# Chunked attention and two feed-forward layers: one written order for every engine up to the end of block 0

## The chip, the core and the metric

One Trainium2 chip, one of its cores. The time is device microseconds of one execution; the result of a comparison is the median of several runs. TensorE (PE) multiplies, VectorE (DVE) and GpSimd (POOL) do elementwise work, ScalarE (ACT) does exponentials, copies and ReLU, SyncE (SP) issues nearly all transfers.

## The reference

Attention over 4 batches, 8 heads, 768 positions of 64 values, in chunks of 32 positions, each of which sees itself, 16 positions to the left, 8 to the right and 8 memory positions. Its output, 3072 tokens by 512, goes through two feed-forward layers (512 to 2048 to 512):

```python
scores = scale * np.matmul(q_c, k_full.transpose(0, 1, 3, 2))
scores = scores - np.max(scores, axis=-1, keepdims=True)
a = np.exp(scores)
a = a / (np.sum(a, axis=-1, keepdims=True) + 1e-09)
out[:, :, c_start:c_end] = np.matmul(a, v_full)
...
h = x @ w_in            # first layer
r = np.maximum(h, 0.0)
g = s * (r * r) + b
x = g @ w_out
...
h = x @ w_in            # second layer, with its own weights
g = h - np.tanh(h)
return (g @ w_out).astype(np.float32)
```

## The kernel before

Everything is float32 in effect. A product of the feed-forward layers is made of three matmuls (`three`, L106 to L109): weights and inputs are split into a high part and a remainder (low part), and high×high, low×high and high×low are added in PSUM. Weights arrive as 64-bit numbers and are converted on chip (`to_f32`, L111): one ACT copy (L116), then three DVE operations (L117, L118, L121). `make_pair` (L288) follows with the high part on ACT (L293) and the low part on POOL (L294).

Attention works on 24 units of 128 tokens. For one unit `scores` (L193) does 32 small matmuls (S), the mask on DVE (L210), the row maximum on DVE (L215), eight exponentials on ACT (L218) and the division (L223, L224, L226), on DVE for units 0 to 3 and on POOL after. `transposes` (L228) turns the weights with eight PE transposes (T) and two ACT copies (L235); `values` (L239) does 32 matmuls (V) and splits the result into the high part `xh` (ACT, L261) and the low part `xl` (DVE, L262).

Four units make a block of 512 tokens; there are six. The up-projection of the first layer takes 16 tiles per block: `up1_tile` (L324) is 12 matmuls of 128x512, a ReLU on ACT (L334) and a scaled square on DVE (L336). After every four tiles `combine` (L338) makes four differences on POOL (L340), and two transfers store the results. The loop at L544 places attention steps between tiles: `att_step(i)` is T of unit i-1, V of unit i-2 and S of unit i. During blocks 1 to 3 and 5 the conversions of `w_out` are emitted (`load_quadrant`, L354). Then come the down-projection (class `Down`), whose seven products cycle through four pairs of PSUM banks, the second up-projection (L644) and a second `Down`.

The order of the work: from L534 on PE follows the program; for the other engines, DMA issues included, a scheduler chooses the order when the program is built, from times that it computes itself. It may bring work of a later block forward. On the chip each engine then takes its instructions strictly in that order, and one that waits holds all behind it.

Of the kernel before, what the change touches and what calls it, by code (L numbers as in the profile page):

```python
# [8 lines left out]
F32 = mybir.dt.float32  # L9
F32R = mybir.dt.float32r  # L10
# [7 lines left out]
P = 128  # L18
# [15 lines left out]


# [6 lines left out]
def tile_chunk_attention_two_ffn(  # L42
# [50 lines left out]
    def bank(k):  # L93
        return pb[:, 512 * k:512 * (k + 1)]
# [16 lines left out]
    def to_f32(z, raw):  # L111
# [4 lines left out]
        nc.scalar.activation(out=z, in_=hi32.bitcast(F32), func=AF.Copy, scale=2.0 ** -112)  # L116
# [76 lines left out]
    def scores(u):  # L193
# [11 lines left out]
        sm = sm_t[u] = new(A_SM[u % 2], 8 * KE, F32, "sm").rearrange("p (h k) -> p h k", h=8)  # L205
# [8 lines left out]
        nmx = small.tile([P, 8], F32, tag="nmx", name="nmx")  # L214
        nc.vector.tensor_reduce(out=nmx, in_=sm, op=ALU.max, axis=AX.X, negate=True)  # L215
        sums = small.tile([P, 8], F32, tag="sums", name="sums")
        for h in range(8):
            nc.scalar.activation(  # L218
                out=sm[:, h, :], in_=sm[:, h, :], func=AF.Exp,
                bias=nmx[:, h:h + 1], scale=1.0, accum_out=sums[:, h:h + 1],  # L220
            )
        rs = small.tile([P, 8, 1], F32, tag="rs", name="rs")
        nc.vector.tensor_scalar_add(sums, sums, 1e-9)  # L223
        nc.vector.reciprocal(out=rs.rearrange("p h o -> p (h o)"), in_=sums)  # L224
        eng = nc.vector if u < UB else nc.gpsimd
        eng.tensor_tensor(out=sm, in0=sm, in1=rs.to_broadcast([P, 8, KE]), op=ALU.mult)  # L226

    def transposes(u):  # L228
        sm = sm_t.pop(u)
        pt = pt_t[u] = new(A_PT[u % 2], 8 * P, F32, "pt").rearrange("p (h q) -> p h q", h=8)  # L230
        for g in range(2):
            ps = bank(2 + g)
            for r in range(4):
                nc.tensor.transpose(out=ps[0:KE, P * r:P * (r + 1)], in_=sm[:, 4 * g + r, :], identity=ident)  # L234
            nc.scalar.activation(  # L235
                out=pt[0:KE, 4 * g:4 * g + 4, :], in_=ps[0:KE].rearrange("p (r q) -> p r q", r=4), func=AF.Copy
            )

    def values(u):  # L239
        tv = v_t.pop(u).rearrange("p (e h d) -> p e h d", e=2, h=8)  # L240
        pt = pt_t.pop(u)
        ps = bank(4)
        for r in range(4):
            for e in range(2):
                for g in range(2):
                    c0 = P * r + QE * e
                    nc.tensor.matmul(  # L247
                        ps[64 * g:64 * g + 64, c0:c0 + QE],
                        lhsT=tv[0:KE, e, 2 * r + g, :], rhs=pt[0:KE, 4 * g + r, QE * e:QE * (e + 1)],
                        start=True, stop=True,  # L250
                    )
        j = u // UB
# [5 lines left out]
        xh, xl = x_t[j]  # L258
        c0 = P * (u % UB)
        xp = ps.rearrange("p (c q) -> p c q", c=KD)  # L260
        nc.scalar.activation(out=xh[:, :, c0:c0 + P], in_=xp, func=AF.Copy)  # L261
        nc.vector.tensor_tensor(  # L262
            out=xl[:, :, c0:c0 + P], in0=xp, in1=xh[:, :, c0:c0 + P].bitcast(F32), op=ALU.subtract
        )

    done = [0]

    def att_part(part, u):
        if 0 <= u < NU:
            {"S": scores, "T": transposes, "V": values}[part](u)  # L270
            if part == "V":
                done[0] = u + 1
                loads_to(u + 3)

    def att_step(i, parts="TVS"):

        for part in parts:
            att_part(part, i - {"S": 0, "T": 1, "V": 2}[part])
# [18 lines left out]
    raws = {}  # L297
    w_loaded, w_made = [0], [0]

    def w1_load():  # L300
        n = w_loaded[0]
        if n < min(8, w_made[0] + 2):
            raws[n] = load_raw(wi1, n, A_RAW[n % 2])
            w_loaded[0] += 1

    def w1_make():
        n = w_made[0]
        if n in raws:
            make_pair(raws.pop(n), A_Z[n % 2], A_W[n], 1, n)
            w_made[0] += 1  # L310

    loads_to(0, spread=True)
    nc.sync.dma_start(out=s_c, in_=s.partition_broadcast(P))
    nc.sync.dma_start(out=b_c, in_=b.partition_broadcast(P))
    make_identity(nc, ident)
    make_masks()
    loads_to(1, spread=True)
    w1_load()
    loads_to(2, spread=True)
    w1_load()  # L320
# [25 lines left out]
    class Down:  # L346


        def __init__(self, src, zmap, smap, whl, stream, ring, load, view, pick, bias, final):
# [3 lines left out]
            self.loaded = 0  # L353
# [136 lines left out]
    def final1(name, g, ps):  # L490
# [44 lines left out]
    w1_make()
    for n, group in enumerate(("S0 S1 S2", "T0 V0 S3", "T1 V1", "T2 S4 V2", "T3 V3")):
        for step in group.split():
            att_part(step[0], int(step[1:]))
        if n:
            w1_load()  # L540
            w1_make()

    thunks = []
    for j in range(NBLK):  # L544
        first = UB * (j + 1) + 2
        steps = [(i, "TVS") for i in range(first, first + UB)] if j + 1 < NBLK else []
        if j == 0:
            steps.insert(0, (first - 1, "TS"))
        at_tile = {16 * n // len(steps): step for n, step in enumerate(steps)}
        for q in range(4):  # L550
            oa, ob = (
                new(A_OT[q % 2][h], 4 * NB, F32, ("oa", "ob")[h]).rearrange("p (s k t) -> p s k t", s=4, k=2)
                for h in range(2)
            )
            for i4, (k, i) in enumerate(((0, 0), (0, 1), (1, 0), (1, 1))):
                if j == 0:
                    w1_load()
                    while w_made[0] <= min(2 * q + k + 1, 7):
                        w1_load()
                        w1_make()  # L560
                up1_tile(j, 2 * q + k + 8 * i, oa[:, 2 * i:2 * i + 2, k, :])
                if 4 * q + i4 in at_tile:
                    att_step(*at_tile[4 * q + i4])
                if (j in (1, 2, 3) and q in (0, 2)) or (j == NBLK - 1 and q in (0, 1)):
                    if i4 == 1:
                        thunks.append(down1.load_quadrant(A_RAW[1 if j == NBLK - 1 else q // 2]))
                    if i4 == 3:
                        thunks.pop()()
                if j == NBLK - 1 and i4 == 0 and q in (1, 2):
                    down1.weights(0, q - 1)  # L570
                    down1.load_to(q - 1)
            combine(*(t.rearrange("p s k t -> p s (k t)") for t in (oa, ob)), nc.gpsimd)
            nc.sync.dma_start(out=o1[j][:, q, 0:3], in_=oa[:, 1:4].rearrange("p s k t -> p s (k t)"))
            nc.sync.dma_start(out=o1[j][:, q, 3:7], in_=ob.rearrange("p s k t -> p s (k t)"))
# [36 lines left out]
    def final2(name, g, ps):  # L611
# [29 lines left out]
        None, final2,  # L641
    )

    for n in range(8):  # L644
        for g in range(NG):
# [6 lines left out]
            for i in range(2):  # L652
                ps = bank2((2 * at_ + i) % 4)
# [93 lines left out]
```

## Time and profile before

| | |
|---|---|
| median of three runs | 1133.98 us (1132.64 to 1134.48) |
| the profiled execution | 1133.25 us; its span, first to last instruction, 1131.5 us |
| busy: PE, DVE, ACT, POOL | 1072.5, 638.5, 488.7, 453.7 us |
| mean granted TensorE clock | 0.98 |
| qk load of one unit, v load, weight load | 640 KB, 384 KB, 1024 KB |

In the rows below, an instruction of the time line begins with its start and its duration in us; then come engine, line, operation, output<-inputs, shapes and count, and in brackets the idle time before it with what ended it. Groups by line give the busy time in us and the mean in ns behind the bar, then idle time before them. PEclk is the granted clock: 1.00 is 2.4 GHz, 0.5 is 1.2 GHz.

### The profile page before, as it was taken

The page shows a single profiled execution, that of the slowest core. Times are in us where ns is not written, and L with a number is a line of the kernel's source. Part 1 is how long each engine was busy: PE and PEld are TensorE (multiplying, and loading weights), DVE is VectorE, ACT ScalarE, POOL GpSimd, SP SyncE. Part 2 cuts the span into 40 slices and gives each one's busy share as a digit, 9 for nine tenths or more (in the row PEclk, how much of TensorE's full clock was granted, in tenths as well). Part 3 has the DMA queues.
Part 4 walks back from the last instruction along what each step waited for, and adds up shares of the span by engine and source line. Part 5 has one row for each costly group of instructions (what it writes and reads, how often), then busy time and mean ns, then how long its engine had stood idle before and what let it go on. Part 6 is the DMA issues. An engine that isn't in the chain of part 4 may idle for free.

```text
span 1131.5 us, 15217 instructions
## 1 busy us (share of the span) xinstructions
PE 1072.5 (95%) x6048; PEld 886.1 (78%) x6048; DVE 638.5 (56%) x610; ACT 488.7 (43%) x863; POOL 453.7 (40%) x296
## 2 busy tenths in 40 slices
PE   4467999999999999999999999999999999999998
PEld 3346888888888888888888788888888888888886
DVE  5987444444455356657778886333322366667654
ACT  5644544444453345445555433222222354444432
POOL 2343444444448734110110158666655852011100
PEclk9678999999999999999999999999999999999999
DMA  8665755555545675655655686655544885567661
GB/s 306 223 224 197 260 204 205 205 205 212 189 189 211 243 263 186 202 186 187 204 202 189 223 268 237 238 205 197 224 164 168 307 282 201 186 207 251 237 215 56
DMA packets 71686, 242.15 MB, mean 214 GB/s; under 512 B 5312, under 2 KB 5312, under 8 KB 61376
## 3 DMA queue, kind: packets, MB, share of 16 engines
q1 hardware_dynamic: 71280, 240.01, 59.3%
q10 hardware_dynamic: 336, 1.18, 0.3%
q8 instruction: 47, 0.77, 0.3%
q14 instruction: 23, 0.19, 0.1%
HBM read 146.80 MB, written 94.37 MB: 213 GB/s over the span
## 4 chain that ended last, share of the span: by engine, by line
PE 88%; DVE 6%; DMA 3%; ACT 2%; issue 1%; POOL 0%; SPq 0%; POOLq 0%; ACTq 0%
PE pb L107 28%; PE pb L109 28%; PE pb L108 28%; DMA raw<-in_wo_dram 2%; PE pb L247 2%; DVE z L118 1%; PE pb L234 1%; PE pb L201 1%; ACT sm L218 1%; DMA qk<-in_qk_dram 1%; DVE z L121 1%; DVE z L117 1%; ACT zq L116 1%; DVE sm L210 1%; DVE nmx L215 0%
## 5 line engine op out<-in xcount | busy, mean ns | idle before, releaser
L109 PE MATMUL pb<-ringhringl,whl 128*128 128x512 f32 x560 | 218.0, 389 | 0.0
L107 PE MATMUL pb<-ringhringl,whl 128*128 128x512 f32 x560 | 217.9, 389 | 0.0
L108 PE MATMUL pb<-ringhringl,whl 128*128 128x512 f32 x560 | 217.9, 389 | 0.0
L431 DVE TENSOR_TENSOR ringhringl<-part,ringhringl 128x1024 fp32r<-128x1024 f32 x92 | 129.0, 1404 | 84.1 <-ACT ringhringl L430 83.8
L340 POOL TENSOR_TENSOR ob<-oa 128x512 f32<-128x512 f32 x96 | 136.4, 1422 | 65.0 <-DVE oa L660 40.0
L430 ACT ACTIVATE ringhringl<-part 128x1024 fp32r<-128x1024 f32 x92 | 97.7, 1061 | 135.5 <-PE pb L109 122.6
L107 PE MATMUL pb<-xh,w 128*128 128x512 f32 x384 | 153.0, 399 | 2.0 <-ACT xh L261 1.7
L109 PE MATMUL pb<-xl,w 128*128 128x512 f32 x384 | 150.8, 393 | 2.9 <-DVE xl L262 2.9
L108 PE MATMUL pb<-xh,w 128*128 128x512 f32 x384 | 150.6, 392 | 0.0
L109 PEld LDWEIGHTS pb<-ringhringl,whl 128*128 128x128 f32 x560 | 105.1, 188 | 22.3 <-DVE ringhringl L426 0.3
L336 DVE SCALAR_TENSOR_TENSOR oa<-pb,s_c,r 128x512 f32<-128x512 f32 x96 | 70.4, 748 | 92.2 <-ACT r L334 87.9
L108 PEld LDWEIGHTS pb<-ringhringl,whl 128*128 128x128 f32 x560 | 105.1, 188 | 21.9
L107 PEld LDWEIGHTS pb<-ringhringl,whl 128*128 128x128 f32 x560 | 105.1, 188 | 21.7
L660 DVE TENSOR_TENSOR oa<-pb,r 128x1024 f32<-128x1024 f32 x48 | 58.4, 1220 | 110.3 <-ACT r L659 101.6
L659 ACT ACTIVATE r<-pb 128x1024 f32<-128x1024 f32 x48 | 49.1, 1025 | 132.8 <-PE pb L109 128.8
L334 ACT ACTIVATE r<-pb 128x512 f32<-128x512 f32 x96 | 54.8, 589 | 103.7 <-PE pb L109 103.7
L412 POOL TENSOR_TENSOR whl<-s,whl 128x1024 fp32r<-128x1024 f32 x16 | 41.5, 2592 | 135.1 <-ACT whl L411 135.1
L218 ACT ACTIVATE sm<-sm,nmx 128x96 f32<-128x96 f32 x192 | 69.2, 362 | 60.0 <-DVE nmx L215 60.0
L426 DVE SCALAR_TENSOR_TENSOR ringhringl<-part,b_c,ringhringl 128x1024 fp32r<-128x1024 f32 x48 | 71.4, 1494 | 37.5 <-ACT ringhringl L425 37.5
L340 POOL TENSOR_TENSOR ob<-oa,ob 128x512 f32<-128x512 f32 x48 | 64.1, 1336 | 66.6 <-DVE oa L660 45.7
L107 PE MATMUL pb<-x2hx2l,w 128*128 128x512 f32 x224 | 87.3, 390 | 2.4 <-DVE sumU L498 2.4
L107 PEld LDWEIGHTS pb<-xh,w 128*128 128x128 f32 x384 | 72.6, 189 | 19.5 <-ACT xh L261 1.9
(100 smaller groups left out, 1888.3 us busy)
## 6 DMA issues: line engine op xcount, KB each, us to landing
o<-ob SPq DMA_DIRECT2D x48, 1024.0 KB, 5.2
part<-o SPq DMA_DIRECT2D x84, 512.0 KB, 4.5
part<-o SPq DMA_DIRECT2D x42, 1024.0 KB, 5.1
o<-oa SPq DMA_DIRECT2D x48, 768.0 KB, 3.3
raw<-in_wi_dram SPq DMA_DIRECT2D x16, 1024.0 KB, 5.9
raw<-in_wo_dram SPq DMA_DIRECT2D x16, 1024.0 KB, 6.1
qk<-in_qk_dram SPq DMA_DIRECT2D x24, 640.0 KB, 6.9
v<-in_vw_dram SPq DMA_DIRECT2D x21, 384.0 KB, 3.5
```

Source lines behind the costliest of these rows:

```text
L107: nc.tensor.matmul(acc, lhsT=whi, rhs=xhi, start=first, stop=False)
L108: nc.tensor.matmul(acc, lhsT=wlo, rhs=xhi, start=False, stop=False)
L109: nc.tensor.matmul(acc, lhsT=whi, rhs=xlo, start=False, stop=last)
L218: nc.scalar.activation(out=sm[:, h, :], in_=sm[:, h, :], func=AF.Exp, bias=nmx[:, h:h + 1], scale=1.0, accum_out=sums[:, h:h + 1],)
L334: nc.scalar.activation(out=r, in_=ps, func=AF.Relu)
L336: nc.vector.scalar_tensor_tensor(out=dst, in0=ps2, scalar=s_c[:, 0:1], in1=r2, op0=ALU.mult, op1=ALU.mult)
L340: sub = lambda o, x, y: eng.tensor_tensor(out=o, in0=x, in1=y, op=ALU.subtract)
L426: nc.vector.scalar_tensor_tensor(out=xl, in0=src, scalar=self.bias, in1=xh.bitcast(F32), op0=ALU.add, op1=ALU.subtract)
L430: nc.scalar.activation(out=xh, in_=src, func=AF.Copy)
L431: nc.vector.tensor_tensor(out=xl, in0=src, in1=xh.bitcast(F32), op=ALU.subtract)
L659: nc.scalar.activation(out=r, in_=ps[:, :, 0:NB], func=AF.Tanh)
L660: nc.vector.tensor_tensor(out=oa[:, 2 * i:2 * i + 2], in0=ps[:, :, 0:NB], in1=r, op=ALU.subtract)
```

## The change

Up to the end of block 0 every engine follows one written list, `START`. Its tokens name a step and a unit, weight piece, tile or group: `qk`, `vv`, `ra` load; `S M R E D` are scores, mask, maximum, exponentials, division; `T C V X L` are transposes, their copies, values, `xh` and `xl`; `z o h l` are the four stages of a weight piece (ACT copy, three DVE operations, high part, low part); `F r Q` are a tile's products, ReLU and square; `K st` are the combination and its stores. The list holds attention units 0 to 7 whole; the scores of units 8 and 9 and the transposes of unit 8, which stood in block 0 before, come in block 1.

With it: low parts of the first layer's `w_in` go from POOL to DVE; divisions of units 4 to 7 too; of block 0's four combinations the first two go to DVE. The first five qk loads have buffers of their own, and v loads are issued by SP (before, the first three by ACT). Block 1 holds six attention steps, at tiles 0, 2, 5, 8, 11 and 14. The conversions of `w_out` are emitted in blocks 2 to 4 and 5. The second layer's PSUM bank pairs are moved on by one (`turn`).

```diff
+START = """
+qk0 qk1 qk2 S0 M0 qk3 R0 S1 M1 E0 qk4 R1 S2 M2 ra0 E1 S3 D0 R2 M3 vv0 E2 D1 S4 ra1 T0 R3 M4 C0 D2
+vv1 z0 T1 R4 V0 qk5 C1 o0 T2 X0 z1 vv2 E3 qk6 L0 o1 V1 vv3 S5 X1 ra2 C2 L1 D3 V2 ra3 X2 M5 T3 L2 S6
+C3 R5 h0 V3 M6 vv6 l0 X3 h1 vv5 L3 z2 R6 F0 E4 l1 o2 F1 r0 z3 D4 h2 ra4 F2 r1 Q0 E5 o3 F3 qk7 r2 l2
+vv4 Q1 T4 r3 ra5 D5 h3 F4 E6 Q2 Q3 l3 F5 K0 z4 C4 F6 r4 o4 r5 st0 T5 r6 Q4 h4 S7 Q6 z5 V4 Q5 F7 l4
+ra6 o5 F8 qk8 D6 h5 C5 M7 F9 qk9 X4 l5 r7 r8 L4 vv7 Q7 T6 r9 Q8 V5 C6 K1 F10 z6 vv9 X5 Q9 ra7 R7 F11
+o6 E7 st1 L5 h6 D7 V6 r10 z7 l6 T7 X6 Q10 r11 F12 C7 o7 F13 Q11 h7 L6 K2 r12 l7 V7 r13 Q13 F14 Q12
+X7 vv8 L7 F15 r14 st2 r15 Q15 Q14 K3 st3
+"""
...
+    A_QK0 = ("Q0", "Q1", "Q2", "E14", "E16", "Q0", "Q1", "Q2")
+    A_V0 = ("Z0", "Z1", "Z2", "Z9", "Z10", "Z0", "Z1", "Z2")
+    A_SM0 = ("S0", "S1", "Z7", "Z8") * 2
...
-        eng = nc.vector if u < UB else nc.gpsimd
+        eng = nc.vector if u < 8 else nc.gpsimd
         eng.tensor_tensor(out=sm, in0=sm, in1=rs.to_broadcast([P, 8, KE]), op=ALU.mult)
...
+    def w1_low(n):
+        hi, lo = (w1_w[n][:, 1024 * k:1024 * (k + 1)] for k in range(2))
+        nc.vector.tensor_tensor(out=lo, in0=w1_z.pop(n), in1=hi.bitcast(F32), op=ALU.subtract)
...
-            ps = bank2((p * NG + g) % 4)
+            ps = bank2((p * NG + g + self.turn) % 4)
...
+        "K": lambda q: up1_combine(0, q, nc.vector if q < 2 else nc.gpsimd), "st": lambda q: up1_store(0, q),
+    }
+    with tc.manual_schedule():
+        for token in START.split():
+            name = token.rstrip("0123456789")
+            steps[name](int(token[len(name):]))
+            if token == "qk2":
+                nc.sync.dma_start(out=s_c, in_=s.partition_broadcast(P))
+                nc.sync.dma_start(out=b_c, in_=b.partition_broadcast(P))
+
     ctx.enter_context(tc.manual_schedule(engines={nc.tensor.engine}))
...
+    att = {(1, t): 8 + n for n, t in enumerate((0, 2, 5, 8, 11, 14))}
+    att.update({(j, 4 * n): 4 * j + 6 + n for j in range(2, NBLK - 1) for n in range(4)})
...
+            if (j, t) in att:
+                att_step(att[j, t])
+            up1_products(j, t)
+            up1_relu(j, t)
+            up1_square(j, t)
+            if (j in (2, 3, 4) and q in (0, 2)) or (j == NBLK - 1 and q in (0, 1)):
...
-                ps = bank2((2 * at_ + i) % 4)
+                ps = bank2((2 * at_ + i + 1) % 4)
```

## Rows read from the trace of the kernel before

**Rows 1.** The page's slices: 40 equal parts of the span, in tenths
```profile
PE   4467999999999999999999999999999999999998
PEclk9678999999999999999999999999999999999999
```
**Rows 2.** Windows, 30 to 40 us: PE, PEld, DVE, ACT, POOL, clock, DMA share, GB/s
```profile
30.00:40.00 10.00, 5.08 (x64) 4.41 (x68) 9.93 (x9) 5.00 (x15) 5.10 (x2) 0.54 0.74 275
```
**Rows 3.** Waits, 0 to 115 us: who for whom, us, times, longest
```profile
ACT zq L116 <- DMA raw<-in_wo_dram: 13.4, 4, 6.0
PE pb L234 <- POOL sm L226: 13.1, 2, 7.4
```
**Rows 4.** Groups by line and shape, 0 to 113 us
```profile
L294 POOL TENSOR_TENSOR w<-z,w 128x1024 fp32r<-128x1024 f32 x8 | 20.9, 2612 | 43.2 <-ACT w L293 43.2
L118 DVE SCALAR_TENSOR_TENSOR z<-raw,z 128x1024 int32<-128x1024 int32 x8 | 16.8, 2102 | 0.1
L215 DVE TENSOR_REDUCE nmx<-sm 128x8 f32<-128x768 f32 x8 | 7.6, 946 | 0.1
L336 DVE SCALAR_TENSOR_TENSOR oa<-pb,s_c,r 128x512 f32<-128x512 f32 x7 | 5.2, 739 | 2.9 <-ACT r L334 2.9
L262 DVE TENSOR_TENSOR xl<-pb,xh 128x512 fp32r<-128x512 f32 x6 | 4.0, 673 | 0.0
L226 DVE TENSOR_TENSOR sm<-sm,rs 128x768 f32<-128x768 f32 x4 | 3.8, 952 | 0.0
L224 DVE RECIPROCAL rs<-sums 128x8 f32<-128x8 f32 x7 | 1.4, 198 | 0.1
L223 DVE TENSOR_SCALAR sums<-sums 128x8 f32<-128x8 f32 x7 | 1.2, 167 | 5.6 <-ACT sm L218 5.6
```
**Rows 5.** Time line of DVE, 8 to 37 us
```profile
8.23 1.02 DVE L210 SCALAR_TENSOR_TENSOR sm<-pb,mask_first 128x384 f32<-128x384 f32 x2 [8.23 <-PE pb L201]
...
33.10 1.23 DVE L118 SCALAR_TENSOR_TENSOR z<-raw,z 128x1024 int32<-128x1024 int32 x1
...
34.36 1.23 DVE L121 SCALAR_TENSOR_TENSOR z<-raw,z 128x1024 int32<-128x1024 int32 x1
...
36.44 0.68 DVE L117 TENSOR_SCALAR z<-z 128x1024 int32<-128x1024 int32 x1
```
**Rows 6.** The page's costliest groups, whole span
```profile
L660 DVE TENSOR_TENSOR oa<-pb,r 128x1024 f32<-128x1024 f32 x48 | 58.4, 1220 | 110.3 <-ACT r L659 101.6
L340 POOL TENSOR_TENSOR ob<-oa 128x512 f32<-128x512 f32 x96 | 136.4, 1422 | 65.0 <-DVE oa L660 40.0
```
**Rows 7.** DMA issues, 0 to 115 us: KB each, median us to landing
```profile
v<-in_vw_dram ACTq DMA_DIRECT2D x3, 384.0 KB, 7.6
```
**Rows 8.** The chain that ended last, 120 to 133 us: start, us, what
```profile
130.15 0.87 PE pb L234 x8
131.02 1.08 PE pb L247 x32
132.10 0.82 PE pb L201 x32
132.92 0.43 PE pb L107
```
**Rows 9.** Time line of PE and POOL, 6 to 142 us
```profile
6.54 1.56 PE L201 MATMUL pb<-qk 64*64 64x96 f32 x32 [6.54 <-DMA qk<-in_qk_dram]
...
63.31 0.63 PE L108 MATMUL pb<-xh,w 128*128 128x512 f32 x1
...
63.74 0.63 PE L109 MATMUL pb<-xl,w 128*128 128x512 f32 x1
...
139.06 1.47 POOL L226 TENSOR_TENSOR sm<-sm,rs 128x768 f32<-128x768 f32 x1 [4.61 <-ACT r L334]
...
141.15 0.39 PE L107 MATMUL pb<-xh,w 128*128 128x512 f32 x1
```
**Rows 10.** PE's waits from 118 us to the end
```profile
PE pb L107 <- DVE sumU L498: 2.4, 1, 2.4
```

More of the change, by code (lines that the diff above doesn't have):

```diff
@@ L109, in three, with scaled, filled @@
         nc.tensor.matmul(acc, lhsT=whi, rhs=xlo, start=False, stop=last)
-    def to_f32(z, raw):
+    def scaled(z, raw):
+        hi32 = raw.rearrange("p (n two) -> p n two", two=2)[:, :, 1]
+        nc.scalar.activation(out=z, in_=hi32.bitcast(F32), func=AF.Copy, scale=2.0 ** -112)
+    def filled(z, raw):
         pair = raw.rearrange("p (n two) -> p n two", two=2)
@@ L123, in to_f32 @@
         )
+    def to_f32(z, raw):
+        scaled(z, raw)
+        filled(z, raw)
     A_W = [f"E{n}" for n in range(8)]
@@ L213, in scores, with maximum, exponentials @@
             )
-        nmx = small.tile([P, 8], F32, tag="nmx", name="nmx")
-        nc.vector.tensor_reduce(out=nmx, in_=sm, op=ALU.max, axis=AX.X, negate=True)
-        sums = small.tile([P, 8], F32, tag="sums", name="sums")
+    def maximum(u):
+        nmx = mx_t[u] = small.tile([P, 8], F32, tag="nmx", name="nmx")
+        nc.vector.tensor_reduce(out=nmx, in_=sm_t[u], op=ALU.max, axis=AX.X, negate=True)
+    def exponentials(u):
+        sm, nmx = sm_t[u], mx_t.pop(u)
+        sums = sum_t[u] = small.tile([P, 8], F32, tag="sums", name="sums")
         for h in range(8):
@@ L221, in scores, with divide @@
             )
+    def divide(u):
+        sm, sums = sm_t[u], sum_t.pop(u)
         rs = small.tile([P, 8, 1], F32, tag="rs", name="rs")
@@ L229, in transposes, with copies @@
         sm = sm_t.pop(u)
+        for g in range(2):
+            for r in range(4):
+                nc.tensor.transpose(
+                    out=bank(2 + g)[0:KE, P * r:P * (r + 1)], in_=sm[:, 4 * g + r, :], identity=ident
+                )
+    def copies(u):
         pt = pt_t[u] = new(A_PT[u % 2], 8 * P, F32, "pt").rearrange("p (h q) -> p h q", h=8)
         for g in range(2):
-            ps = bank(2 + g)
-            for r in range(4):
-                nc.tensor.transpose(out=ps[0:KE, P * r:P * (r + 1)], in_=sm[:, 4 * g + r, :], identity=ident)
             nc.scalar.activation(
-                out=pt[0:KE, 4 * g:4 * g + 4, :], in_=ps[0:KE].rearrange("p (r q) -> p r q", r=4), func=AF.Copy
+                out=pt[0:KE, 4 * g:4 * g + 4, :], in_=bank(2 + g)[0:KE].rearrange("p (r q) -> p r q", r=4),
+                func=AF.Copy,
             )
@@ L257, in values, with x_high, x_low, att_step @@
             )
-        xh, xl = x_t[j]
         c0 = P * (u % UB)
[L260 to L278, printed above, removed]
+        return [t[:, :, c0:c0 + P] for t in x_t[j]] + [bank(4).rearrange("p (c q) -> p c q", c=KD)]
+    def x_high(u):
+        xh, xl, xp = x_parts(u)
+        nc.scalar.activation(out=xh, in_=xp, func=AF.Copy)
+    def x_low(u):
+        xh, xl, xp = x_parts(u)
+        nc.vector.tensor_tensor(out=xl, in0=xp, in1=xh.bitcast(F32), op=ALU.subtract)
+    def att_step(i):
+        if 2 * UB <= i - 1 < NU:
+            transposes(i - 1)
+            copies(i - 1)
+        if 2 * UB <= i - 2 < NU:
+            values(i - 2)
+            x_high(i - 2)
+            x_low(i - 2)
+            if i + 1 < NU:
+                load_v(i + 1)
+        if i < NU:
+            scores(i)
+            if i + 3 < NU:
+                load_qk(i + 3)
+            mask(i)
+            maximum(i)
+            exponentials(i)
+            divide(i)
     wi = {}
@@ L314, in tile_chunk_attention_two_ffn, with w1_load, w1_scaled, w1_filled @@
-    nc.sync.dma_start(out=b_c, in_=b.partition_broadcast(P))
+    raws, w1_z, w1_w = {}, {}, {}
+    def w1_load(n):
+        raws[n] = load_raw(wi1, n, A_RAW[n % 2])
+    def w1_scaled(n):
+        w1_z[n] = new(A_Z[n % 2], 1024, F32, "z")
+        scaled(w1_z[n], raws[n])
+    def w1_filled(n):
+        filled(w1_z[n], raws.pop(n))
+    def w1_high(n):
+        w1_w[n] = new(A_W[n], 2048, F32R, "w")
+        nc.scalar.activation(out=w1_w[n][:, 0:1024], in_=w1_z[n], func=AF.Copy)
+    def w1_low(n):
+        hi, lo = (w1_w[n][:, 1024 * k:1024 * (k + 1)] for k in range(2))
+        nc.vector.tensor_tensor(out=lo, in0=w1_z.pop(n), in1=hi.bitcast(F32), op=ALU.subtract)
+        wi[1, n] = tuple(t.rearrange("p (i c m) -> p i c m", i=2, c=KD) for t in (hi, lo))
@@ new lines, in up1_square @@
+    def up1_square(j, t):
+        q, k, i = t // 4, t // 2 % 2, t % 2
+        if (j, q) not in oab:
+            oab[j, q] = tuple(
+                new(A_OT[q % 2][h], 4 * NB, F32, ("oa", "ob")[h]).rearrange("p (s k t) -> p s k t", s=4, k=2)
+                for h in range(2)
+            )
+        ps2, r2 = (x.rearrange("p (n t) -> p n t", n=2) for x in (up_ps.pop((j, t)), up_r.pop((j, t))))
+        nc.vector.scalar_tensor_tensor(
+            out=oab[j, q][0][:, 2 * i:2 * i + 2, k, :], in0=ps2, scalar=s_c[:, 0:1], in1=r2,
+            op0=ALU.mult, op1=ALU.mult,
+        )
@@ L338, in combine, with up1_combine, up1_store @@
+    def up1_combine(j, q, eng):
+        combine(*(t.rearrange("p s k t -> p s (k t)") for t in oab[j, q]), eng)
+    def up1_store(j, q):
+        oa, ob = oab.pop((j, q))
+        nc.sync.dma_start(out=o1[j][:, q, 0:3], in_=oa[:, 1:4].rearrange("p s k t -> p s (k t)"))
+        nc.sync.dma_start(out=o1[j][:, q, 3:7], in_=ob.rearrange("p s k t -> p s (k t)"))
     def combine(oa, ob, eng):
@@ L529, in tile_chunk_attention_two_ffn @@
         lambda t: lambda k: t[:, :, HB * k:HB * (k + 1)],
-        b_c[:, 0:1], final1,
+        b_c[:, 0:1], final1, 0,
     )
-    ctx.enter_context(tc.manual_schedule(engines={nc.tensor.engine}))
[L535 to L541, printed above, removed]
-    thunks = []
[L544 to L574, printed above, removed]
@@ new lines, in tile_chunk_attention_two_ffn @@
+    steps = {
+        "qk": load_qk, "vv": load_v, "S": scores, "M": mask, "R": maximum, "E": exponentials, "D": divide,
+        "T": transposes, "C": copies, "V": values, "X": x_high, "L": x_low,
+        "ra": w1_load, "z": w1_scaled, "o": w1_filled, "h": w1_high, "l": w1_low,
+        "F": lambda t: up1_products(0, t), "r": lambda t: up1_relu(0, t), "Q": lambda t: up1_square(0, t),
+        "K": lambda q: up1_combine(0, q, nc.vector if q < 2 else nc.gpsimd), "st": lambda q: up1_store(0, q),
+    }
@@ new lines, in tile_chunk_attention_two_ffn @@
+    load_qk(10)
+    load_v(10)
+    thunks = []
+    for j in range(1, NBLK):
+        for t in range(16):
+            q, i4 = t // 4, t % 4
+            if (j, t) in att:
[4 more added lines that the diff above has]
+            if (j in (2, 3, 4) and q in (0, 2)) or (j == NBLK - 1 and q in (0, 1)):
+                if i4 == 1:
+                    thunks.append(down1.load_quadrant(A_RAW[1 if j == NBLK - 1 else q // 2]))
+                if i4 == 3:
+                    thunks.pop()()
+            if j == NBLK - 1 and i4 == 0 and q in (1, 2):
+                down1.weights(0, q - 1)
+                down1.load_to(q - 1)
+            if i4 == 3:
+                up1_combine(j, q, nc.gpsimd)
+                up1_store(j, q)
```

65 lines of the change are left out of this document (21 added, 44 removed).

## The prediction
> **What bounds the kernel now.** The page's slices come first. PE stands at 9 from the fifth slice on, and its granted clock at full; only in the first four (some 113 us) is it lower, with PEclk at 9, 6, 7 and 8 [rows 1]. After 118 us PE's wait list holds one wait of size, 2.4 us [rows 10]. So the remaining order is bound by PE, and what can be won lies before about 140 us.
>
> What bounds that start? In the window from 30 to 40 us DVE is busy 9.93 of 10 us, PE 5.08, ACT 5.00, POOL 5.10, and the TensorE clock is at 0.54 on the mean, that is mostly at 1.2 GHz [rows 2]. DVE is full, but not with useful time alone. The same DVE operation on 128x1024 integers, L118, takes 1.23 us at 33.10 while POOL rests [rows 5], but 2.10 us on the mean of its eight, among which POOL makes low parts of 2.61 us each [rows 4]. I read this as POOL holding DVE up. Later in the start the waits change: ACT stood 13.4 us before conversions of `w_out` whose transfers hadn't landed, and PE 13.1 us before transposes for divisions by POOL [rows 3]. That work had been brought forward from later blocks, and what queued behind it on ACT were copies and ReLUs that PE needed.
>
> **A mark to measure from.** Before, the three last tiles of block 0 run from 132.92 [rows 8] to 141.15 [rows 9], where block 1's first tile begins: 8.23 us, 2.74 us a tile. By then PE has also done the scores of units 8 and 9 and the transposes of unit 8, which the change does after its F15. These are 2×0.82 + 0.87 = 2.5 us [rows 8], so the mark before is 141.15 − 2.5 = 138.6. If the end of F15 comes at X after the change, the span becomes X + (1131.5 − 138.6) = X + 992.9, corrected by what changes later.
>
> **X, by DVE's work.** Everything in the list that is DVE's, at undisturbed durations:
> - masks 8 × 1.02 (one unit is two instructions) = 8.2 [rows 5]; maxima 8 × 0.946 = 7.6; divisions 8 × (0.167 + 0.198 + 0.952) = 10.5; remainders `xl` 8 × 0.673 = 5.4; squares 16 × 0.739 = 11.8 [rows 4].
> - three operations of a weight piece, 8 × (0.68 + 1.23 + 1.23) = 25.1 [rows 5].
> - low parts, now on DVE: not seen there. Below stands the 1.22 of DVE's other 128x1024 operation with two inputs, above POOL's own 2.61 [rows 6, 4]. I take 1.22, same engine and size: 8 × 1.22 = 9.8 (20.9 at the upper end).
> - two combinations, 8 instructions of 128x512: between the 0.673 of `xl` [rows 4], of this size, and POOL's 1.42 [rows 6]. I take 0.67: 5.4 (11.4).
>
> The sum is 83.8 us. The last two squares follow F15, so 82.3 lie before. POOL has no work in this stretch until the third combination, so undisturbed durations apply; if they did not, L118's excess alone is 8 × (2.10 − 1.23) = 7.0 us.
>
> DVE started at 8.23 [rows 5], because the first scores began at 6.54 [rows 9]. Three v loads of 384 KB, issued by ACT, went beside the 640 KB of that first qk load [rows 7]; they now come after five qk loads. I credit 1.2 us and start at 7.0 (bounds 6 and 8.2).
>
> DVE's waits inside the list are the least certain term. In the first 20 us it follows ACT and PE round the attention chain, unit by unit, and waits some 4 us. Later the list mostly puts a step of another unit or piece between a step and the one that needs it; I allow 5 us for that whole stretch. So 9 us in all, with 4 and 22 as ends: 4 is the chain's start alone, 22 has the clock case below and a late transfer in it. After the last `xl`, V7's copy and remainder are passed and F14 and F15 run: 2 × 2.74 from V7's end, less 1.9 us for X7 and L7, is 3.6. X = 7.0 + 82.3 + 9 + 3.6 = 101.9.
>
> **X, by PE's work.** F0 needs L3 and low part 0. Ahead of these DVE has 7 masks, 6 maxima, 4 divisions, 2 weight pieces, 1 low part and 4 remainders: 7.1 + 5.7 + 5.3 + 6.3 + 1.2 + 2.7 = 28.3 us, so F0 starts near 7 + 28.3 + 4 = 39. From there PE has 16 × 2.74 + 4 × (0.87 + 1.08) + 0.82 = 52.5 us at full clock [rows 8], and would end at 92. Before it, 62 to 68 us was back to back work at starts 0.43 us apart [rows 9], the lower level, 5.2 us a tile; such a rise costs some 3 us. PE thus has about 7 us to spare against DVE. Both engines are nearly full, so a stall of either comes through after that.
>
> **After block 0.** (1) Unit 8's scores now come first in block 1, and its transposes two tiles later, after 5.5 us. The chain from scores to the end of the division took 139.06 + 1.47 − 132.92 = 7.6 us before [rows 8, 9]. That makes PE wait 2.1 us. Also the fourth combination is queued on POOL ahead of that division: four instructions of 1.42 us [rows 6], 5.7 us, started 2.3 us after F15. It ends 8 us after F15, about when the division is ready (0.82 + 6.1 = 6.9 us); some 1.1 us more. I take 3.5, bounds 2 and 10 (POOL slowed by DVE, and `w_out` conversions taken forward into block 1, each waiting on its transfer at the head of ACT). The later steps stand three tiles apart, 8.2 us, and fit. (2) `turn`: the wait of 2.4 us at the second up-projection's first tile, on the last sums that read the PSUM pair it starts in [rows 10], goes, since it now starts in the next pair. Late next is nothing that I see; −2.4, bounds 0 and −2.4. (3) `w_out` later: in blocks 2 to 5 PE is the bound and ACT and DVE have room; 0, at worst the 1 or 2 us of a late first weight. SP's v issues and POOL's free time cost nothing: neither ends a chain there.
>
> **Sum.** 101.9 + 992.9 + 3.5 − 2.4 = 1095.9 us of span. The profiled execution took 1133.25 around a span of 1131.5, 1.75 more, so 1097.7; the median of the runs shown is 0.7 above that execution, so 1098.4. I forecast 1098: 36 us faster.
>
> **Rivals.**
> - *The clock stays down longer.* For: mean 0.54 in rows 2, and PE waits for DVE in every attention chain. Against: PE's work ahead of F0 at the slow rate is 7 × 1.56 [rows 9] + 4 × 2 × (0.87 + 1.08) = 26.5 us in 34, denser than the 5 in 10 of before, and from F0 on it is dense. If full clock comes only at 70 us, as before (68), 31 us at half rate lose 15.5 of PE's work; less the 7 to spare and 1 or 2 more lost beside it, X is 10 later: 1108.
> - *One late transfer holds everything.* SP issues in list order, so weight loads 6 and 7 stand behind stores and behind v loads that wait for a V. In order engines pass a late landing on to all. For: 13.4 us of such waits [rows 3]. Against: those were loads that came forward; here loads are asked for long before use, but ra7 closely. One such case costs two landings of about 5 us: 1108.
> - *Block 1 starves* for the reason under (1), at its upper bound and once more for unit 9: 1108 to 1110.
> - *Slower: the lower clock level up to F15.* Three PSUM banks serve the tiles, so PE can be stopped briefly after each one by a late square. If that kept the clock at 1.2 GHz throughout, PE's 52.5 us become 105, from F0 at 39: X = 144 and the time 1098 + 42 = 1140, slower by 6. It decides from X = 138 on. Against: from slice 5 on the same three banks run at full clock [rows 1]. The Trainium skill, "TensorE: Matmul & The Clock Gate", section "A second HAM failure mode: psum-queue depth-cycling", tells of a kernel in which short idle times between groups, while cycling through PSUM banks, made the clock oscillate; by it half of block 0 would run slow. An oscillation of half the time would give 1119.
> - *The list doesn't bind*, and the scheduler's order stands: then low parts and divisions alone move, and DVE is relieved of waits but not of `w_out` work: 1120 or above.
>
> **How the numbers follow.** The forecast holds 0.66 (its own range 1090 to 1104), the clock 0.10, a late transfer 0.10, block 1 0.05, oscillation or an unbound list 0.04, the full slower case and unforeseen stalls of that size 0.04, and no change, by several in part, 0.01. About 0.2% is what a measurement tells from no change. The range runs from 1088 (waits of 4 us, a start 1 us earlier, a last wait 2 us shorter in block 1, and 2 us for sizes) to 1115, past the three cases at 1108; it leaves out what lies beyond. Faster 0.94, same 0.01, slower 0.05.
>
> **What would show it.** Right: F15 ends between 95 and 110 us; L118 and L121 near 1.2 us throughout; low parts near 1.2 on DVE; DVE over 90% busy from 20 to 95; full clock from 50 at the latest; a short wait of the ninth unit's transposes for POOL; none at the second up-projection. Wrong: a PEclk of 0.5 past 70 us, ACT or PE waiting on `qk`, `v` or `raw` transfers for more than 5 us after 20 us, or PE waits in blocks 1 to 5.

## The result

The changed kernel takes 1101.38 us (1099.57 to 1102.74, 4 runs) where the kernel before takes 1134.23 (1132.64 to 1134.99, 4 runs) on the same chip: ratio 0.971, 95% interval 0.969 to 0.973, faster by 33 us. The forecast was 1098 us, between 1088 and 1115. The profiled execution took 1099.57 us around a span of 1097.8.

The page's slices of the changed kernel, 27.4 us each, beside [rows 1]:
```profile
PE   5999799999999999999999999999999999999998
PEclk9899999999999999999999999999999999999999
```
PE is dense from the second slice on instead of the fifth; one slice, the fifth (110 to 137 us), has a hole. The same window as [rows 2], and the stretch from the first mask to the last `xl` of block 0 (columns as there):
```profile
6.47:95.44 88.97, 77.50 (x758) 62.23 (x758) 84.24 (x117) 63.65 (x200) 9.21 (x5) 0.94 0.85 287
30.00:40.00 10.00, 8.68 (x115) 6.72 (x116) 9.89 (x16) 8.05 (x24) 0.00 (x0) 0.83 1.00 309
```
DVE is full as before, but PE beside it is busy 8.68 of 10 us instead of 5.08, and POOL is at rest. Over the whole stretch DVE is busy 84.24 of 88.97 us: it is still the fullest engine, now with useful time. The groups that answer to [rows 4], 0 to 113 us:
```profile
L360 DVE TENSOR_TENSOR w<-z,w 128x1024 fp32r<-128x1024 f32 x8 | 10.8, 1351 | 0.0
L132 DVE SCALAR_TENSOR_TENSOR z<-raw,z 128x1024 int32<-128x1024 int32 x8 | 10.8, 1345 | 0.3
L131 DVE TENSOR_SCALAR z<-z 128x1024 int32<-128x1024 int32 x8 | 5.5, 684 | 0.0
L405 DVE TENSOR_TENSOR ob<-oa 128x512 f32<-128x512 f32 x4 | 2.7, 684 | 0.0
```
L132 is the L118 of before: 1.35 us on the mean, not 2.10. A low part takes 1.35 on DVE, not 2.61 on POOL; a combination's instruction takes the 0.68 that were put down for it. PE's waits from 0 to 125 us (the first five and two more), then all from 125 us to the end:
```profile
PE pb L221 <- DMA qk<-in_qk_dram: 4.8, 1, 4.8
PE pb L281 <- DVE xl L303: 3.4, 1, 3.4
PE pb L221 <- DVE sm L232: 3.1, 4, 1.1
PE pb L262 <- POOL sm L256: 3.1, 1, 3.1
PE pb L262 <- DVE sm L256: 2.0, 1, 2.0
PE pb L117 <- DVE oa L390: 1.3, 2, 0.9
PE pb L118 <- DVE w L360: 1.3, 2, 1.1
...
PE pb L262 <- POOL sm L256: 4.7, 2, 2.7
```
The 13.1 us for divisions by POOL [rows 3] are 3.1 now, plus 4.7 later; the 2.4 at the second up-projection [rows 10] is gone. One line is hardly better than before, ACT's waits from 0 to 125 us:
```profile
ACT zq L124 <- DMA raw<-in_wo_dram: 10.8, 5, 4.3
```
These are conversions of `w_out`, which the changed program emits only from block 2 on. The scheduler still takes them forward, into the stretch of the written list itself, and with them the scores of unit 8. The time line of the changed kernel near the end of block 0:
```profile
76.77 0.33 SPq L330 DMA_DIRECT2D raw<-in_wo_dram  x1
77.56 0.56 PE L221 MATMUL pb<-qk 64*64 64x96 f32 x14
...
90.66 2.45 POOL L256 TENSOR_TENSOR sm<-sm,rs 128x768 f32<-128x768 f32 x1
91.71 2.49 DVE L132 SCALAR_TENSOR_TENSOR zq<-raw,zq 128x1024 int32<-128x1024 int32 x1
91.84 0.50 PE L118 MATMUL pb<-xh,w 128*128 128x512 f32 x1 [1.05 <-DVE w L360]
95.00 0.47 PE L117 MATMUL pb<-xh,w 128*128 128x512 f32 x1 [0.37 <-DVE oa L390]
95.28 1.14 ACT L124 ACTIVATE zq<-raw 128x1024 f32<-128x1024 f32 x1 [4.29 <-DMA raw<-in_wo_dram]
97.77 0.40 PE L117 MATMUL pb<-xh,w 128*128 128x512 f32 x1
```
At 76.77 SP asks for the first `w_out` piece, at 77.56 PE computes the last of unit 8's scores (the first began at 69.45), at 90.66 POOL divides them, at 91.71 DVE converts `w_out`, and at 95.28 ACT has stood 4.29 us before a piece that hadn't landed. F15 begins at 95.00 and ends when block 1's first tile begins, at 97.77: so the list sets the order of what is in it, but it is no wall against what stands behind it.

### The profile page after: what moved, and what is told of

The parts are those of the page before. It is cut to its first block, busy times and chain, and to the rows that moved or that the text cites. A ratio compares the mean times of both kernels' runs of the same rounds, so it can differ in the third digit from the quotient of the medians.

```text
span 1097.8 us, 15240 instructions
## 1 busy us (share of the span) xinstructions
PE 1067.6 (97%) x6048; PEld 880.9 (80%) x6048; DVE 642.2 (58%) x630; ACT 488.0 (44%) x863; POOL 425.9 (39%) x276
## 4 chain that ended last, share of the span: by engine, by line
PE 90%; DVE 6%; DMA 2%; issue 1%; ACT 1%; POOL 0%; POOLq 0%; ACTq 0%; SPq 0%; DVEq 0%
PE pb L117 29%; PE pb L119 29%; PE pb L118 28%; DMA raw<-in_wo_dram 2%; PE pb L221 2%; PE pb L281 1%; PE pb L262 1%; DVE zq L132 1%; DVE sm L232 1%; DVE nmx L239 1%; DVE z L132 0%; DVE oa L390 0%; DVE xl L303 0%; DMA qk<-in_qk_dram 0%; DVE z L135 0%
## 5 line engine op out<-in xcount | busy, mean ns | idle before, releaser
L118 PE MATMUL pb<-ringhringl,whl 128*128 128x512 f32 x560 | 217.8, 389 | 0.0
L405 POOL TENSOR_TENSOR ob<-oa 128x512 f32<-128x512 f32 x92 | 133.9, 1456 | 165.6 <-DVE oa L390 124.7
L118 PE MATMUL pb<-xh,w 128*128 128x512 f32 x384 | 150.6, 392 | 1.3 <-DVE w L360 1.3
L118 PEld LDWEIGHTS pb<-ringhringl,whl 128*128 128x128 f32 x560 | 105.1, 188 | 21.9
```

The lines of the kernel that those rows point to most:

```text
L118: nc.tensor.matmul(acc, lhsT=wlo, rhs=xhi, start=False, stop=False)
L405: sub = lambda o, x, y: eng.tensor_tensor(out=o, in0=x, in1=y, op=ALU.subtract)
```

## The experiments

Each kernel changes the one named, in runs beside the kernel before (1134.4 to 1135.0 us in these runs).

**How much of it is the written order?** The list binds PE alone; placement of work on engines stays.
```diff
-    with tc.manual_schedule():
+    with tc.manual_schedule(engines={nc.tensor.engine}):
```


> The changed kernel with the written list binding PE alone; the scheduler orders DVE, ACT, POOL and SP, all else as changed. Theory: with low parts and divisions on DVE most of the gain is there, but the free order puts weight pieces ahead of the attention chain and the first tile starts later: 1106 to 1118 us. Rival one: the engines' assignment is all of it: 1098 to 1104 us. Rival two: the list is all of it: 1126 to 1136 us.

1124.35 us, ratio 0.991 (0.990 to 0.993): 23 of the 33 us are gone, a figure that lies between those of the theory and of the second rival. PE's largest waits, 0 to 125 us:
```profile
PE pb L221 <- DVE sm L232: 11.1, 6, 5.2
PE pb L281 <- DVE xl L303: 9.6, 2, 8.6
```
The window from 30 to 40 us (columns as in [rows 2]):
```profile
30.00:40.00 10.00, 4.51 (x48) 3.77 (x48) 5.76 (x9) 5.30 (x16) 0.00 (x0) 0.83 0.92 343
```
POOL is at rest here too, yet DVE is busy only 5.76 of 10 us: ACT stands 14.9 us in all before pieces of `w_in` that haven't landed, and what DVE and PE need of it for the attention chain comes behind that. F0 begins at 61.19 us instead of 35.15.

**Whose order?** PE, DVE, ACT and POOL bound, SP's transfers free.
```diff
+    with tc.manual_schedule(engines={nc.tensor.engine, nc.vector.engine, nc.scalar.engine, nc.gpsimd.engine}):
```


> The changed kernel, but in the start's list SP alone is free: the scheduler chooses the order of the transfers that SP issues, while PE, DVE, ACT and POOL keep the written order. With only PE bound the time was 1124.35, 23 us above the changed kernel. Theory: those 23 us are the order of DVE and ACT (conversions of w_out taken forward ahead of ReLUs, copies and low parts); with these bound, SP's own order matters little, since loads are asked for long before use: 1099 to 1104. Rival: the order of the loads carries a large part of it (weight loads and loads of w_out beside qk and v loads that are wanted first): 1110 to 1125, with PE or DVE waits on qk, v or raw transfers of more than 5 us in the first 60 us.

1104.19 us (1102.49 to 1105.71), ratio 0.973 (0.972 to 0.974): 0.2 us above the theory's range, and the rival's time is out, though its sign was there: PE waits 9.1 us on qk transfers up to 60 us instead of 4.8, and F0 begins at 39.53. So some 20 of the 23 us are the order on the computing engines and about 3 that of the loads; these 3 are near the noise, since the interval of this ratio overlaps that of the changed kernel.

**Low parts back on POOL**, all else as changed.
```diff
-        nc.vector.tensor_tensor(out=lo, in0=w1_z.pop(n), in1=hi.bitcast(F32), op=ALU.subtract)
+        nc.gpsimd.tensor_tensor(out=lo, in0=w1_z.pop(n), in1=hi.bitcast(F32), op=ALU.subtract)
```


> The changed kernel with the eight low parts of w_in back on POOL. Theory: POOL's two-input work holds DVE's up, so the three conversion operations go back to about 1.2, 2.1 and 1.5 us in the mean, 13 us more on DVE for the 10.8 us taken off it, and the low parts come later: 1104 to 1112 us. Rival: DVE only counts its own work, so 10.8 us less on it makes the start shorter: 1091 to 1097 us.

1108.51 us, ratio 0.978 (0.976 to 0.979): 7 us worse. The groups, 0 to 113 us:
```profile
L360 POOL TENSOR_TENSOR w<-z,w 128x1024 fp32r<-128x1024 f32 x8 | 20.8, 2605 | 60.6 <-ACT w L356 60.6
L132 DVE SCALAR_TENSOR_TENSOR z<-raw,z 128x1024 int32<-128x1024 int32 x8 | 10.8, 1347 | 0.3
L131 DVE TENSOR_SCALAR z<-z 128x1024 int32<-128x1024 int32 x8 | 10.5, 1315 | 1.6 <-ACT z L124 1.6
```
Only L131 grew, from 0.68 to 1.32 us; L132 and L135 (1.23) didn't, against what was expected. The time line says why. It shows POOL's low part and DVE's next L131:
```profile
44.48 2.41 POOL L360 TENSOR_TENSOR w<-z,w 128x1024 fp32r<-128x1024 f32 x1 [4.24 <-ACT w L356]
45.20 2.24 DVE L131 TENSOR_SCALAR z<-z 128x1024 int32<-128x1024 int32 x1
```
POOL ends at 46.89, L131 at 47.44, 0.55 later; alone it takes 0.68. DVE's operation does its work when POOL's is over: it is held, not slowed, and which one is held depends on which begins meanwhile. The Trainium skill says so, "SBUF — State Buffer", section "Who interferes with whom": the two engines share a port pair by an exclusive lock, and of two operations that use it the later one blocks; the trace agrees here to 0.13 us (46.89 + 0.68 = 47.57 against 47.44). It is not one lucky case: in this kernel and in the one below with divisions back on POOL, all ten L131 that begin beside an operation of POOL in the first 113 us end 0.55 us behind it, whatever their duration (0.85 to 2.24 us).

DVE lost 5 us by it (8 × 0.63). But it was freed of 10.8 us of low parts, so the expected sum, 13 us more for 10.8 less, is not what made this kernel slower. PE waited 5.7 us for three low parts that came late; the last stood on POOL behind the third combination, and the clock fell behind that wait (0.66 from 90 to 100 us). The wait, and the end of block 0:
```profile
93.75 0.79 PE L118 MATMUL pb<-xh,w 128*128 128x512 f32 x1 [4.31 <-POOL w L360]
101.06 0.39 PE L117 MATMUL pb<-xh,w 128*128 128x512 f32 x1
```
Block 1's first tile begins 3.3 us later than in the changed kernel (97.77). The other 5.1 us by which the profiled spans differ come after that: PE waits 6.6 us for POOL's division of unit 9 instead of 3.1, with the clock at 0.66 from 120 to 130 us. So the time came as forecast, by late results more than by a fuller DVE.

**Low parts on DVE alone**, in the kernel before (`make_pair` with its low part on DVE for `w_in`).

> The kernel before with one part of the change alone: the eight low parts of w_in on DVE. Theory: it takes the hold-up of DVE's conversions away (13 us of DVE) and adds 10 us of low parts, so the start shortens by what the undo of this part cost, 3 to 8 us: 1126 to 1131 us. Rival: without a written order the extra DVE work lengthens the attention chain, 1134 to 1142 us.

1130.43 us, ratio 0.9966 (0.9953 to 0.9979): 4 us better, in the theory's range. L118 fell to 1.21 us, yet PE's wait for divisions by POOL was 14.3 us: without the order the rest stays.

**Divisions of units 4 to 7 and two combinations back on POOL**, all else as changed.
```diff
-        eng = nc.vector if u < 8 else nc.gpsimd
+        eng = nc.vector if u < UB else nc.gpsimd
...
-        "K": lambda q: up1_combine(0, q, nc.vector if q < 2 else nc.gpsimd), "st": lambda q: up1_store(0, q),
+        "K": lambda q: up1_combine(0, q, nc.gpsimd), "st": lambda q: up1_store(0, q),
```


> The changed kernel with divisions of units 4 to 7 and the first two combinations back on POOL. Theory: DVE gets 9 us less work of its own, and POOL's 16 us of two-input work hold it up for about as long; the divisions are 0.5 us slower each and queue behind combinations: 1100 to 1108 us. Rival: they are hidden behind other work and DVE gains: 1092 to 1098 us.

1100.51 us, ratio 0.970 (0.968 to 0.972), as the changed kernel. The groups, 0 to 113 us:
```profile
L360 DVE TENSOR_TENSOR w<-z,w 128x1024 fp32r<-128x1024 f32 x8 | 12.8, 1600 | 0.2 <-ACT w L356 0.2
L132 DVE SCALAR_TENSOR_TENSOR z<-raw,z 128x1024 int32<-128x1024 int32 x8 | 12.7, 1591 | 0.3
L131 DVE TENSOR_SCALAR z<-z 128x1024 int32<-128x1024 int32 x8 | 8.0, 996 | 1.3 <-ACT z L124 1.3
```
Against the changed kernel these three grow by 2.0 + 1.9 + 2.5 = 6.4 us. Of the 9 us that DVE hands to POOL it loses at least 6.4 in being held. The rest does show at the end of block 0, where block 1's first tile begins 3.2 us earlier than in the changed kernel (97.77):
```profile
94.56 0.39 PE L117 MATMUL pb<-xh,w 128*128 128x512 f32 x1
```
What follows takes 5.0 us more in the profiled execution: PE's waits for divisions by POOL are 8.8 us there instead of 7.8, and the clock falls three times (0.83 from 110 to 120 and from 140 to 150 us, 0.88 and 0.94 from 160 to 180) instead of once. So this part of the change is worth nothing from end to end; the 3 us that POOL could save in block 0 are lost in block 1.

**Holding `w_out` back.** In the changed kernel each transfer of `w_out` is made to wait for a result of the block where it is emitted: DVE first copies one column of `oa` into the buffer.
```diff
+            nc.vector.tensor_copy(out=raw[:, 0:1].bitcast(F32), in_=after)
```


> The changed kernel in which each transfer of w_out waits, by a copy of one column into its buffer, for the square beside which it is emitted (blocks 2 to 5). Theory: the 10 us that PE still loses between 90 and 170 us come from w_out conversions taken forward: low part 7 is on time and PE's waits for POOL's divisions in block 1 shrink from 7.8 us to under 2: 1090 to 1096 us. Rival: they come from block 1's six attention steps and POOL's combinations; the waits stay at 6 us or more: 1098 to 1103 us.

1095.72 us, ratio 0.966 (0.965 to 0.967): 5.7 us better. PE waits for nothing between 98 and 125 us; later for POOL 4.5 us in six waits, the longest 2.00 (at 156.92). So the waits for POOL's divisions fell from 7.8 us to 4.5, not under 2 as the theory had it. In the profiled executions block 0 ends 1.0 us earlier (96.78) and block 2 begins 8.7 us earlier (160.84 against 169.49). Of that 4.7 us are lost again later, where `w_out` is now converted, and the spans differ by 4.0.

**The same gate in the kernel before**, and then with the conversion emitted half a block behind its transfer.

> The kernel before, with the same gate on its w_out transfers (blocks 1 to 3 and 5). Theory: conversions taken forward cost the start before 10 to 20 us, by waits of ACT on transfers and of PE behind it: 1113 to 1124 us. Rival: they only filled time that the low parts on POOL had already lost: 1129 to 1135 us.

> The kernel before with the gate on w_out, and each conversion emitted half a block after its transfer instead of two tiles. Theory: in the first gated run block 0 ended some 19 us earlier, but ACT then waited 6 us at the head of its queue for each transfer and PE lost 12 us and clock; with time for the transfer that goes: 1113 to 1122 us. Rival: the gate itself costs what it wins: 1129 us or more.

1137.12 us (1129.40 to 1142.01, 7 runs), ratio 1.0025 (1.0000 to 1.0049), and 1136.33 (1130.82 to 1139.60, 10 runs), ratio 1.0006 (0.9987 to 1.0024): no gain, though block 0 ended some 19 us earlier (the transposes of unit 8 at 111.0 and 111.6, before at 130.15). What was won was lost again after that. The first time lies above both of its ranges, the second in its rival's. The profile of the first is of an execution of 1129.40 us, so it doesn't show what brings the median to 1137.12; that of the second is of one of 1138.19. In the second, the time line of one conversion:
```profile
187.39 0.33 SPq L287 DMA_DIRECT2D raw<-in_wo_dram  x1
195.09 1.12 ACT L116 ACTIVATE zq<-raw 128x1024 f32<-128x1024 f32 x1 [6.83 <-DMA raw<-in_wo_dram]
```
PE's largest wait there, from 125 us on:
```profile
PE pb L107 <- DVE oa L338: 15.3, 8, 3.6
```
The transfer is issued at 187.39, and after one copy, at 187.67, ACT's next instruction is its conversion: it stands 6.83 us with exponentials and ReLUs behind it, and PE stops for squares. Emitting the conversion later didn't part the two: the scheduler put it right behind the transfer again. So what `w_out` taken forward costs the kernel before, net, stays open: the gate that removes it brings a price of the same size.

**The changed kernel with gate, lag, and block 1's steps at tiles 0, 1, 4, 7, 10, 13.** Gate and lag are as above; the edit of the steps:
```diff
-    att = {(1, t): 8 + n for n, t in enumerate((0, 2, 5, 8, 11, 14))}
+    att = {(1, t): 8 + n for n, t in enumerate((0, 1, 4, 7, 10, 13))}
```


> The changed kernel with the gate on w_out, conversions half a block after their transfers, and block 1's attention steps at tiles 0, 1, 4, 7, 10 and 13, so that three tiles stand between all but the first two, whose scores come early. Theory: the wait of 2.0 us and the stretch at half clock at 157 us go, which came from a step two tiles behind another: 1090 to 1094 us. Rival: unit 8 is then asked for too early and PE waits there instead: 1096 to 1100 us.

1091.12 us (1090.90 to 1092.03), ratio 0.962 (0.961 to 0.963): the fastest of all, 10 us below the changed kernel. All of PE's waits from 125 us on:
```profile
PE pb L262 <- POOL sm L256: 2.5, 5, 0.6
PE pb L117 <- DVE oa L392: 0.4, 1, 0.4
```
The longest is 0.6 us, and the granted clock isn't below 1.00 in any 10 us from 40 us on.

**The bank shift undone.**
```diff
-            ps = bank2((p * NG + g + self.turn) % 4)
+            ps = bank2((p * NG + g) % 4)
...
-                ps = bank2((2 * at_ + i + 1) % 4)
+                ps = bank2((2 * at_ + i) % 4)
```


> The changed kernel with the shift of the second layer's PSUM pairs taken back. Theory (the prediction's term of 2.4 us): the second up-projection's first tile starts again in the pair that the last sums are read from, PE waits there some 2.4 us, and the time rises by that much: 1103 to 1105, ratio to the changed kernel 1.002. Rival: the wait comes back but something else after it absorbs it, or it does not come back: 1100.5 to 1102.

1105.50 us (1104.76 to 1110.09), ratio 0.9755 (0.974 to 0.977): 4.1 above the changed kernel's median (5.0 by the ratios to the kernel before), more than the 2.4 expected; the rival is out. The wait:
```profile
607.16 0.65 PE L117 MATMUL pb<-x2hx2l,w 128*128 128x512 f32 x1 [2.40 <-DVE sumU L563]
```
The windows from there (columns as in [rows 2]; the clock is third from the end):
```profile
600.00:610.00 10.00, 7.60 (x29) 5.85 (x28) 7.83 (x9) 2.17 (x2) 0.00 (x0) 0.87 0.81 310
610.00:620.00 10.00, 10.00 (x43) 8.19 (x43) 6.83 (x7) 3.29 (x4) 1.30 (x1) 0.96 0.62 216
```
The 2.4 us are back, and behind them the clock stood lower, at 0.87 and 0.96, which costs another 1.3 + 0.4 us. A wait of 2.00 us at 166.77, which the changed kernel has at 166.58 too, was followed by the same here (0.85 and 0.98 from 160 to 180 us, 1.7 us) and by a clock of 1.00 there. 2.4 + 1.7 + 1.7 = 5.8, the difference of the two profiled spans being 5.9 (1103.7 and 1097.8).

## Why the prediction was right, and where it was not

**X came 4.1 us earlier than forecast.** By the terms of the prediction, measured in the changed kernel's time line and in DVE's groups from 6.47 us to the last `xl` (90.3 us of busy time, added up group by group):

| term | forecast | measured |
|---|---|---|
| DVE's first mask | 7.0 | 6.5 |
| the list's operations at undisturbed durations | 82.3 | 82.2 |
| overlap of neighbours | 0 | -5.4 |
| unit 8 and `w_out`, on DVE inside the list | 0 | 6.1 |
| held by POOL | 0 | 2.0 |
| waits | 9 | 4.7 |
| end of the last `xl` | 98.3 | 96.1 |
| from there to the end of F15 | 3.6 | 1.7 |
| X | 101.9 | 97.8 |

The durations were right nearly to the digit. What the sum of durations hides is that an instruction begins before its neighbour has ended:
```profile
66.39 1.22 DVE L360 TENSOR_TENSOR w<-z,w 128x1024 fp32r<-128x1024 f32 x1
67.53 0.68 DVE L303 TENSOR_TENSOR xl<-pb,xh 128x512 fp32r<-128x512 f32 x1
```
The first ends at 67.61, the second has begun at 67.53. This makes 5.4 us (what is left of 6.5 + 90.3 + 4.7 over 96.1); neighbours inside one group are already merged in the 90.3, and the 117 durations one by one make 91.2. The held time is two operations beside POOL's third combination: one L132 of 2.19 us and one L360 of 2.30, where 1.23 and 1.22 are undisturbed; before that combination, where POOL had no work, the durations were undisturbed, as forecast. F0 began at 35.15, not 39. The first scores began at 4.78 instead of 6.54, 1.8 us earlier where 1.2 were credited; that the later v loads are the reason was not tried by itself.

What the list did not name cost PE a stop inside it too. Unit 8's mask and maximum got between the steps of unit 7's division on DVE, and PE stood before unit 7's transposes:
```profile
78.16 1.02 DVE L232 SCALAR_TENSOR_TENSOR sm<-pb,mask_mid 128x384 f32<-128x384 f32 x2 [0.78 <-PE pb L221]
...
79.21 0.95 DVE L239 TENSOR_REDUCE nmx<-sm 128x8 f32<-128x768 f32 x1
80.08 0.95 DVE L256 TENSOR_TENSOR sm<-sm,rs 128x768 f32<-128x768 f32 x1
...
81.18 1.91 PE L262 MATMUL pb<-ident,sm 128*96 128x128 f32 x8 [1.98 <-DVE sm L256]
```
Behind that stop the clock was at 0.83 from 80 to 90 us, 1.7 us of work. The kernel with `w_out` held back keeps the stop (1.92 us at 82.28), so it isn't `w_out`'s.

**The loss after X was 10.4 us instead of 3.5: this step failed.** It is a wait of 0.9 for a square at 101.8, 3.1 for the division of unit 9 with 1.7 us of lower clock behind it (0.93 and 0.90 from 110 to 130 us), and 4.7 in two more for POOL (2.71 at 133.57 and 2.01 at 166.58). The time line of the changed kernel there:
```profile
106.20 2.25 DVE L132 SCALAR_TENSOR_TENSOR zq<-raw,zq 128x1024 int32<-128x1024 int32 x1
...
112.02 0.38 ACT L245 ACTIVATE sm<-sm,nmx 128x96 f32<-128x96 f32 x1 [1.86 <-DVE nmx L239]
...
113.85 2.17 POOL L405 TENSOR_TENSOR ob<-oa 128x512 f32<-128x512 f32 x1 [6.49 <-DVE oa L390]
115.03 1.02 DVE L253 TENSOR_SCALAR sums<-sums 128x8 f32<-128x8 f32 x1
...
117.99 1.43 PE L262 MATMUL pb<-ident,sm 128*96 128x128 f32 x8 [3.09 <-POOL sm L256]
118.31 1.14 ACT L124 ACTIVATE zq<-raw 128x1024 f32<-128x1024 f32 x1 [2.36 <-DMA raw<-in_wo_dram]
```
Unit 9's scores were done soon after 106, but its mask waited on DVE behind a conversion of `w_out` (106.20), and even L253, the first small step of its division, took 1.02 us beside POOL's combination, where it takes 0.16 alone.

Reason (1) of the prediction failed in its place: unit 8's scores had come forward into block 0, and its transposes at 104.66 waited for nothing. "The later steps stand three tiles apart, 8.2 us, and fit" failed too: units 9 and 10 stand so, and PE waited 3.1 and 2.71 us for them. Step (3) failed in its premise: `w_out` is emitted later, yet six of its eight pieces were converted between 87 and 124 us, and the seventh was asked for at 131.63. The prediction had this as the upper end of (1), at 10 us, and gave its rival on block 1 5 in 100. That it is the cause is shown: with the transfers held back, 98 to 125 us holds no wait of PE, and 5.7 us come back. A gap of two tiles between steps is the rest: it stands where the prediction didn't look, between tile 14 of block 1 and tile 0 of block 2. The 2.1 us that were worked out for such a gap at unit 8 came there as 2.01 (at 166.58). With block 1's steps moved and the lagged conversion 4.6 us more came back; 3.7 of these are the wait of 2.00 us at 156.92 in the gated kernel and 1.7 us of lower clock behind it (0.93 and 0.90 from 150 to 170 us). The lag was not tried by itself, but each conversion of that run begins within 0.1 us of its transfer's landing, as without the lag, so nothing in the trace speaks for it.

**The turn** gave the 2.4 us forecast, and up to 4.1 where the clock falls behind the wait.

**Sum.** 97.8 + 992.9 + 10.4 - 2.4 = 1098.7 against a span of 1097.8. Of the 0.9 us left, 0.8 are the scores of unit 8 [rows 8]: PE had done them before X, and the mark of 992.9 counts them behind it. Errors of -4.1 and +6.9 us nearly cancelled: that the forecast was closer than its terms is luck.

**The rivals.** Full clock came at 40 us, not at 70; after that it fell behind two stops, at 81.2 and 118.0 us. No transfer that the list names held it up: PE's only wait for one is the first, 4.8 us, and ACT's for pieces of `w_in` are 1.4 us in all. The list does bind what is in it. The slower rival, the lower level up to F15 by stops at three PSUM banks, is out: the granted clock is 1.00 in each 10 us from 40 to 80 us, with these three banks in use. The Trainium skill, "TensorE: Matmul & The Clock Gate", section "A second HAM failure mode: psum-queue depth-cycling", describes a clock that oscillates behind short idle times between groups; the changed kernel shows none in this stretch. Where its clock fell after 40 us, PE had stood 2.0 us (81.2) or 3.1 us (118.0) just before. (The 1119 for an oscillation of half the time is the middle of 1098 and 1140. By the rival's own terms, 78.8 us of tiles from F0 at 39, X would be 117.8 and the time 1114.) Of the prediction's signs of error two did appear, ACT's wait on `raw` of over 5 us and PE waits in block 1.

**What the parts are worth.** Undone one at a time: the written order 23 us (some 3 of them SP's), low parts on DVE 7, the turn 4, divisions and combinations nothing; together 34, of 33 measured. That the sum fits proves little: in the kernel before, low parts on DVE gave 4, so the parts are not quite independent. The buffers of the first qk loads, the v loads on SP, block 1's six steps and the later emission of `w_out` were not undone by themselves.

## What to carry to other kernels

Where two engines hold each other up, durations alone don't price an operation moved between them. Count also what the other engine loses, and when the result is ready: 8 low parts moved to DVE gained 7 us though DVE then had more to do, and four divisions and two combinations gained nothing. A written list orders only what it names; look in the trace for work of later blocks between its steps, and hold that back by its data, on an engine whose queue can bear the wait. Of a step's price ask also whether the clock fell behind the wait that it leaves; the length of the wait alone did not tell here.

## What the hardware showed

- A conversion or low part on DVE (L131, L132, L135, L360) that begins while POOL's runs ends about when it would if it began at POOL's end: 0.55 us after it for an operation of 0.68, 1.08 after it for those of 1.22. This explains stretches from 0.68 to 2.24 us by one rule, without a slower rate. Not every operation is held: masks, maxima, `xl` and squares that began beside POOL's work kept their 0.55, 0.95, 0.68 and 0.74 us.
- POOL is held in the same way. Its division of unit 8 at 90.66 took 2.45 us where 1.47 is undisturbed, beside DVE's L360 that had begun at 89.48 and ended at 91.78; DVE's L132 at 91.71 then took 2.49 and ended 1.09 after that division.
- Neighbouring DVE instructions overlap by some 0.08 us in the records, so a sum of durations is an upper bound (here by 6.3 of 91.2 us). Where the second reads what the first wrote, as L132 behind L131, there is a gap of 0.04 us instead.
- A stop of PE of 2.0 or 2.4 us was followed by a lower clock in some executions (1.7 us lost) and not in others of nearly the same program. A stop of 3.1 us at 118 us was followed by it in both profiles that show it, one of 2.71 us at 133.57 was not in either.
